# A decayed linear attention in blocks of 64 tokens in place of 128, all its products in 64x64 tiles

## The chip, the cores and the metric

The kernel runs on one core of a Trainium2 chip. The metric is the device time of one execution in microseconds (us); three runs before the change gave 229.84, 229.82 and 229.83, median 229.83. The engines are TensorE (PE, with PEld for its weight loads), VectorE (DVE), ScalarE (ACT), GpSimd (POOL) and SyncE (SP), which issues the transfers. Each takes its instructions in the order in which they were written into the program.

## What is computed

The first half is an attention with an exponential decay per head, 4 batches, 8 heads, 768 tokens, head size 64, as a recurrence over blocks. The reference takes blocks of 64 tokens; the result does not depend on the size of the block.

```python
for b in range(nb):
    qb, kb, vb = (q[:, :, sl], k[:, :, sl], v[:, :, sl])
    intra = np.einsum('bhic,bhjc->bhij', qb, kb) * Dmask[None]
    intra = np.einsum('bhij,bhjd->bhid', intra, vb)
    inter = np.einsum('bhid,bhde->bhie', qb * lam_pow[None], kv_state)
    out[:, :, sl] = intra + inter
    kb_dec = kb * rev_pow[None]
    kv_state = lam_block[None, :, None, None] * kv_state + np.einsum('bhsd,bhse->bhde', kb_dec, vb)
```

The second half takes the attention's result x (the heads side by side, 512 wide): a causal convolution over 5 tokens per channel gives a gate through a sigmoid, x @ w_val is multiplied by the gate, and the product goes through w_out. All is fp32; w_val, conv_w and w_out come as float64.

## The kernel before

The four batches are taken in two pairs, the 768 tokens in 6 chunks of 128: 12 steps, numbered i, of one chunk of one pair each. Steps 0 and 6 begin a pair with an empty state, steps 5 and 11 end one.

A step's recurrence on PE has four kinds of products, all fp32. **Scores** (tile s, line 440): keys times queries for each head and batch, contracting over the head size, in 64x64 tiles of PE with 128 or 64 moving columns, since the upper right quarter is zero and left out; they go in two halves of four heads, u = 0 and 1, through one double bank in PSUM. DVE multiplies each half by the decay mask into A (line 452). **State read** (inter, line 476): the decayed queries qd times the state, 128 columns. **A times v** (intra, line 492): contracting over all 128 tokens of the chunk, so in tiles of 128 rows and 64 columns, into the same xp as the state read. **Outer products** (line 510): decayed keys times v, again over 128 tokens, into st; DVE adds it to the faded state (update, lines 517 and 519), POOL fades the state for the next step into sdec (line 522). In each of them the two batches go side by side. ACT (line 394) or POOL (line 397) scales k, POOL scales q (line 405).

After that, ACT copies xp to x, and x is split into a rounded part x_hi (ACT) and the rest x_lo (DVE in steps 0 and 1, POOL later), so that x @ w_val can be done as three products of a faster type (value groups, tile vp, line 639, 24 products each, two groups a step). DVE does the taps of the convolution (line 603), ACT the sigmoid, DVE multiplies the gate in (line 652), ACT and POOL split again, and PE makes the three products with w_out (output groups, tile op, line 700, 12 products of 512 columns each, two a step). The weights are turned from float64 into such pairs at the start by some ten operations on DVE, ACT and POOL for each half of each weight.

What sets the order is a planner (class Plan): every piece of work is added with an engine, an assumed length, what it needs, the buffers it holds, a rank and, for PE, a number for the tile shape. It plays the work through and writes it out in the order in which the pieces started; the engines then keep to that order. PSUM has eight banks: s and xp two each, four single ones (tag u) for st, the convolution, the value groups and the output groups. A wait in the trace comes from this order together with the semaphores.

Of the kernel before, what the change touches and what calls it, by code (L numbers as in the profile page):

```python
# [9 lines left out]
F32 = mybir.dt.float32  # L10
# [6 lines left out]
P = 128  # L17
C = 128
NB2 = 2
# [4 lines left out]
SLOTS = {"ld": 3, "qd": 2, "A": 2, "x": 3, "xs": 2, "g": 2, "val": 4, "hs": 2, "o": 2, "s": 1, "xp": 1, "u": 4}  # L24
# [5 lines left out]
S_OWN = ()  # L30
# [100 lines left out]
def decay_attention_then_gated_conv(  # L131
# [40 lines left out]
    nc.sync.dma_start(lam_bc, lam.partition_broadcast(P))  # L172
    ident = const.tile([P, P], F32, name="ident")
    make_identity(nc, ident)

    swapped = const.tile([P, P], F32, name="swapped")
    for lo in (0, D):
        nc.gpsimd.tensor_copy(swapped[:, lo : lo + D], ident[:, D - lo : P - lo])
# [11 lines left out]

    dmask = const.tile([P, H, C], F32, name="dmask")

    qdec = const.tile([P, H, C], F32, name="qdec")

    state = const.tile([P, H, D], F32, name="state")
    sdec = const.tile([P, H, D], F32, name="sdec")
    rows = lambda n: slice(n * D, (n + 1) * D)


    s_all = psum.tile([P, NB2, HP, C], F32, name="s", bufs=1)  # L200
    for r in range(2):
        nc.vector.memset(s_all[rows(1 - r), :, 2 * r : 2 * r + 2, 0:D], 0.0)
# [6 lines left out]
    def make_dmask(u):  # L209
        for h in range(HP * u, HP * (u + 1)):  # L210
            nc.vector.tensor_tensor_scan(
                out=dmask[:, h, :],
                data0=lam_bc[:, h : h + 1].to_broadcast([P, C]),
                data1=swapped if h // 2 % 2 else ident,
                initial=0.0,
                op0=ALU.mult,
                op1=ALU.add,
            )

    def make_qdec(h):  # L220
        nc.vector.tensor_tensor_scan(  # L221
            out=qdec[:, h, :],
            data0=lam_bc[:, h : h + 1].to_broadcast([P, C]),
            data1=zero,
            initial=1.0,
            op0=ALU.mult,
            op1=ALU.add,
        )

    t_dmask = {u: add("DVE", 2750, lambda u=u: make_dmask(u), rank=-4 + 0.1 * u) for u in range(2)}  # L230
# [153 lines left out]
    for i in range(N):  # L384
# [16 lines left out]
        def scale_q(u, i=i, s=s):  # L401
            if u == 0:
                s["qd"] = buf("qd", "qd", [P, H, C])
# [363 lines left out]
```

## Time and profile before

| what | value |
|---|---|
| median of 3 runs | 229.83 us |
| span of the profiled execution, first to last instruction | 228.2 us |
| PE busy | 211.4 us, 93% |
| weight load (overlaps PE) | 188.0 us |
| DVE, ACT, POOL busy | 142.8, 112.3, 123.4 us |
| granted PE clock over the span | 0.992 |

In the profile a line names the engine, the operation, the tile written and the tiles read, partitions by elements, the number of instructions, the busy time in us, the mean length of one in ns, and after the second bar the idle time of the engine just before them with what ended it. An fp32 product of the program stands as two matmul records and two weight loads. A record's length reaches over the start of the next ones, so lengths of groups are read from start to start, as the chain of waits gives them. The median is 1.6 us over the span.

### The profile page before, as it was taken

The numbers are of one execution on the slowest core, as the hardware profiler recorded it, in microseconds if no ns is written. First come the engines' busy times: TensorE is split into PE (matmuls) and PEld (weight loads), VectorE is DVE, ScalarE is ACT, GpSimd is POOL, SyncE is SP. The second block draws the span as 40 slices with busy tenths as digits, with TensorE's granted clock in tenths as the row PEclk, the third lists the DMA queues.
The fourth block names the chain that finished last, engine by engine and source line by source line (L and its number), as shares of the span: only waits on it lengthen the run. The fifth ranks groups of instructions, "written<-read, shape, count | busy, mean of one in ns | idle before, by whom it ended". The sixth has DMA issues, their size and how long they took to land.

```text
span 228.2 us, 6134 instructions
## 1 busy us (share of the span) xinstructions
PE 211.4 (93%) x2686; PEld 188.0 (82%) x2686; DVE 142.8 (63%) x196; ACT 112.3 (49%) x190; POOL 123.4 (54%) x93
## 2 busy tenths in 40 slices
PE   7598389997999999999999999999998999999994
PEld 6587388996988999987787899979897899999884
DVE  5598979999799859705789992679117931111100
ACT  2178968458992254254377526455253634121222
POOL 1054997555499989999983224443080616222210
PEclk9999889999999999999999999999999999999999
DMA  5999997997367608183111101111111111111122
GB/s 115 425 418 422 419 399 293 418 375 267 155 217 267 258 3 326 47 329 131 49 49 46 49 0 49 50 46 46 46 47 50 46 46 46 49 46 46 49 92 92
DMA packets 8235, 36.07 MB, mean 158 GB/s; under 512 B 1168, under 2 KB 1424, under 8 KB 4880
## 3 DMA queue, kind: packets, MB, share of 16 engines
q1 hardware_dynamic: 8208, 35.68, 40.4%
q8 instruction: 21, 0.34, 0.6%
q14 instruction: 6, 0.05, 0.1%
HBM read 29.38 MB, written 6.29 MB: 156 GB/s over the span
## 4 chain that ended last, share of the span: by engine, by line
PE 78%; DVE 12%; DMA 2%; ACT 2%; issue 2%; POOL 1%; SPq 0%; ACTq 0%; DVEq 0%
PE vp L639 29%; PE op L700 29%; PE s L440 7%; PE xp L492 7%; DVE A L452 5%; PE xp L476 4%; DVE acc L603 3%; PE st L510 3%; DMA ld<-in_qkv 2%; POOL w_m L283 1%; DVE qdec L221 1%; DVE x_lo L569 1%; DVE w_e L276 1%; ACT g L608 1%; DVE g L652 1%
## 5 line engine op out<-in xcount | busy, mean ns | idle before, releaser
L603 DVE SCALAR_TENSOR_TENSOR acc<-x,conv_sb,acc 128x512 f32<-128x512 f32 x96 | 66.4, 749 | 8.5 <-ACT acc L601 8.3
L700 PE MATMUL op<-wo_hi,hs 128*128 128x512 f32 (+1 forms) x200 | 61.3, 389 | 1.0 <-DVE g L652 0.8
L639 PE MATMUL vp<-x_hi,wv_hi 128*128 128x256 f32 x192 | 54.7, 285 | 0.2 <-ACT g L608 0.2
L639 PE MATMUL vp<-x_hi,wv_lo 128*128 128x256 f32 x192 | 53.6, 279 | 0.0
L639 PE MATMUL vp<-x_lo,wv_hi 128*128 128x256 f32 x192 | 53.6, 279 | 0.0
L677 POOL TENSOR_TENSOR hs<-g,hs 128x512 fp32r<-128x512 f32 x24 | 32.8, 1376 | 33.5 <-ACT hs L674 33.4
L652 DVE TENSOR_TENSOR g<-vp,g 128x512 f32<-128x512 f32 x24 | 16.5, 690 | 46.4 <-PE vp L639 36.1
L700 PEld LDWEIGHTS op<-wo_hi,hs 128*128 128x128 f32 x200 | 35.7, 188 | 8.5 <-DVE g L652 1.0
L708 ACT COPY o<-op 128x512 f32<-128x512 f32 (+1 forms) x25 | 14.2, 569 | 56.1 <-PE op L700 46.9
L574 POOL TENSOR_TENSOR x_lo<-x,x_hi 128x1024 fp32r<-128x1024 f32 x10 | 24.5, 2453 | 30.8 <-ACT x_hi L565 30.8
L700 PE MATMUL op<-wo_lo,hs 128*128 128x512 f32 (+1 forms) x100 | 38.6, 386 | 0.0
L639 PEld LDWEIGHTS vp<-x_hi,wv_hi 128*128 128x128 f32 x192 | 36.0, 187 | 2.5 <-issue 1.0
L639 PEld LDWEIGHTS vp<-x_lo,wv_hi 128*128 128x128 f32 x192 | 36.0, 188 | 0.6
L639 PEld LDWEIGHTS vp<-x_hi,wv_lo 128*128 128x128 f32 x192 | 36.1, 188 | 0.0
L405 POOL TENSOR_TENSOR qd<-ld,qdec 128x512 f32<-128x512 f32 x20 | 26.6, 1348 | 16.4 <-DMA ld<-in_qkv 15.8
L452 DVE TENSOR_TENSOR A<-s,dmask 128x1024 f32<-128x1024 f32 x24 | 29.2, 1218 | 9.8 <-PE s L440 7.5
L440 PE MATMUL s<-ld 64*64 64x128 f32 (+1 forms) x768 | 23.5, 265 | 8.5 <-DVE A L452 7.1
L440 PEld LDWEIGHTS s<-ld 64*64 64x64 f32 x768 | 20.2, 144 | 12.8 <-DVE A L452 8.2
L492 PE MATMUL xp<-A,ld 128*64 128x128 f32 x384 | 28.0, 286 | 2.0 <-DVE A L452 1.2
L492 PEld LDWEIGHTS xp<-A,ld 128*64 128x64 f32 x384 | 22.8, 141 | 4.7 <-issue 1.8
L608 ACT ACTIVATE g<-acc 128x512 f32<-128x512 f32 x24 | 14.3, 597 | 17.9 <-DVE acc L603 17.6
L700 PEld LDWEIGHTS op<-wo_lo,hs 128*128 128x128 f32 x100 | 18.8, 188 | 4.2
(52 smaller groups left out, 220.2 us busy)
## 6 DMA issues: line engine op xcount, KB each, us to landing
ld<-in_qkv SPq DMA_DIRECT2D x22, 1024.0 KB, 8.6
out<-o SPq DMA_DIRECT2D x23, 256.0 KB, 2.0
ld<-in_qkv SPq DMA_DIRECT2D x4, 512.0 KB, 6.6
w_raw<-in_w_val SPq DMA_DIRECT2D x2, 1024.0 KB, 10.8
w_raw<-in_w_out SPq DMA_DIRECT2D x2, 1024.0 KB, 12.4
out<-o SPq DMA_DIRECT2D x2, 128.0 KB, 1.7
conv_raw<-in_conv_w SPq DMA_DIRECT2D x1, 20.0 KB, 7.6
lam_bc<-in_lam SPq DMA_DIRECT2D x1, 4.0 KB, 2.6
```

The costliest lines, as they stand in the source:

```text
L405: nc.gpsimd.tensor_tensor(out=s["qd"][:, hs], in0=lds[i]["qT"][:, u], in1=qdec[:, hs], op=ALU.mult)
L440: nc.tensor.matmul(s_all[keys, b, h, lo:], t["kT"][rows(b), u, h, keys], t["qT"][rows(b), u, h, lo:], start=True, stop=True, skip_group_ch ...
L452: nc.vector.tensor_tensor(out=s["A", u].rearrange("p b h i -> p b (h i)"), in0=s_all.rearrange("p b h i -> p b (h i)"), in1=m.rearrange("p ...
L492: nc.tensor.matmul(s["xp"][rows(h % 2), b, h // 2, :], lds[i]["v"][:, b, h * D : (h + 1) * D], s["A", u][:, b, hl, :], start=first and h < ...
L574: nc.gpsimd.tensor_tensor(out=s["x_lo"], in0=s["x"], in1=s["x_hi"].bitcast(F32), op=ALU.subtract)
L603: nc.vector.scalar_tensor_tensor(out=to, in0=src, scalar=w, in1=to, op0=ALU.mult, op1=ALU.add)
L608: nc.scalar.activation(xu[un]["g"][:, ct].rearrange("p u (b i) -> p b u i", b=NB2), xu[un]["acc", ct].rearrange("p b (u i) -> p b u i", u= ...
L639: nc.tensor.matmul(vp[:, f, :], w[:, ct, fs], xx[:, ct, :], start=n_mm == 0, stop=n_mm == 3 * NT - 1,)
L652: nc.vector.tensor_tensor(out=gs(u), in0=val, in1=gs(u), op=ALU.mult)
L677: nc.gpsimd.tensor_tensor(out=s["h_lo"][:, us], in0=gs(u), in1=s["h_hi"][:, us].bitcast(F32), op=ALU.subtract,)
L700: nc.tensor.matmul(op[:, cols], hh[:, ft, ts], w[:, ft, cols], start=n_mm == 0, stop=n_mm == 3 * NT - 1,)
L708: nc.scalar.copy(s["o", b, j][:, cols], s["op", b, j][:, cols])
```

## The change

The recurrence goes in blocks of 64 tokens. A step is still a chunk of 128 tokens of two batches, but it holds two blocks, k = 0 and 1, and the state is updated, faded and read once for each. All products are 64 by 64 with 64 moving columns: scores only within a block (32 products a step, in one piece but for step 0), outer products per block (32), state read per block (32), A times v per block (32). The data are laid out anew on the host, with half of the heads' batches exchanged, so that four tiles at a time work on different rows and columns of PE. Rows of PE that work side by side write different banks of PSUM. For A times v this needs two turns, z = 0 and 1: tiles of the first turn write one arrangement of banks, those of the second the other, and between them a copy of two columns of xp by ACT (turn) makes the second wait for the first.

In PSUM s, st and xp now share two double banks (tag d). States are three buffers instead of one tile that is overwritten. Steps 0 and 6 read a state too, in their second block; steps 5 and 11 update one, after their first.

```diff
-SLOTS = {"ld": 3, "qd": 2, "A": 2, "x": 3, "xs": 2, "g": 2, "val": 4, "hs": 2, "o": 2, "s": 1, "xp": 1, "u": 4}
+SLOTS = {"ld": 3, "qd": 2, "A": 2, "x": 3, "xs": 2, "g": 2, "val": 4, "hs": 2, "o": 2, "state": 3, "d": 2, "u": 4}
...
-    for h in range(H):
-        t_qdec = add("DVE", 400, lambda h=h: make_qdec(h), [t_qdec], rank=0.4)
+    for a in range(2):
+        t_qdec = add("DVE", 1100, lambda a=a: make_qdec(a), [t_qdec], rank=0.4)
+    t_fadew = add("POOL", 150, make_fadew, [t_qdec], rank=0.4)
...
-                for n in range(2):
-                    for lo in (0, D):
-                        for r in range(2):
-                            h, keys = 2 * r + n, rows(1 - r if lo else r)
+                for a in some:
+                    for p in range(2):
+                        for k in range(2):
+                            for c in range(2):
+                                for b in range(NB2):
+                                    nc.tensor.matmul(
+                                        s["s", n][rows(c), b, k, a, seq(p)],
+                                        kT[rows(b), a, c, p, seq(k)], qT[rows(b), a, c, p, seq(k)],
+                                        start=True, stop=True, skip_group_check=True,
+                                    )
...
+            for k in range(blocks):
+                for n in range(4):
+                    for c in range(2):
                         for b in range(NB2):
                             nc.tensor.matmul(
-                                s["so"][b][:, h], t["kT"][rows(b), u, h], t["qT"][rows(b), u, h], start=True, stop=True
+                                s["st"][rows(b), c, k, n, :], k_[rows(c), k, b, n, :], v_[rows(c), k, b, n, :],
+                                start=True, stop=True, skip_group_check=True,
                             )
...
+        for k in range(blocks):
...
+            t_now = add("DVE", 700, step, [t_st, t_now, t_sdec], [st_buf, new_buf], R - 3, name=f"up{i}")
+            if not (last and k == blocks - 1):
+                t_sdec = add("POOL", 1280, fade, [t_now, t_fadew], [new_buf], R, port=True, name=f"fd{i}")
...
+                                nc.tensor.matmul(
+                                    s["xp"][rows(p), b, 2 * (b ^ c) + a, seq(k)],
+                                    s["state", k][rows(b), c, rows(2 * a + p)], s["qd"][rows(b), a, 2 * c + p, seq(k)],
+                                    start=k == 0 and a == 0 and c == 0, stop=False, skip_group_check=True,
                                 )
...
+        def intra(z, i=i, s=s, first=first, open_xp=open_xp):
+            open_xp()
+            for k in range(2):
+                for n in range(4):
                     for b in range(NB2):
+                        a, p = divmod(n, 2)
                         nc.tensor.matmul(
-                            s["xp"][rows(h % 2), b, h // 2, :],
-                            lds[i]["v"][:, b, h * D : (h + 1) * D],
-                            s["A", u][:, b, hl, :],
-                            start=first and h < 2, stop=h >= H - 2, skip_group_check=True,
+                            s["xp"][rows(p), b, 2 * z + a, seq(k)],
+                            lds[i]["v"][rows(b ^ z), k, b, n, :], s["A"][rows(b ^ z), b, k, a, seq(p)],
+                            start=first and z == 0 and k == 0 and a == 0, stop=z == 1 and k == 1, skip_group_check=True,
                         )
...
+        def change(s=s):
+            nc.scalar.copy(turn, s["xp"][:, :, 0, C - 1])
...
+        t_ia = add("PE", 480, lambda f=intra: f(0), [t_from.get(0), *need], on_xp, R, lag=260, mode=2, name=f"ia{i}0")
...
+        t_turn = add("ACT", 200, change, [t_ia, *t_from.values()], [xp_buf], R - 3, name=f"tn{i}")
+        t_in = [add("PE", 480, lambda f=intra: f(1), [t_turn, *need], on_xp, R, lag=260, mode=2, name=f"ia{i}1")]
```

The planner's table changes with the pieces, so the order changes everywhere. Three places show how.

On PE at the start, from the second step's scores on, before (L440 scores, L510 outer products, L476 state read, L492 A times v):

```order
L510 MATMUL st<-ld 64x64 x16
L440 MATMUL s<-ld 64x128 x4
L440 MATMUL s<-ld 64x64 x4
L440 MATMUL s<-ld 64x128 x4
L440 MATMUL s<-ld 64x64 x4
L476 MATMUL xp<-qd,state 64x128 x16
L492 MATMUL xp<-A,ld 64x128 x8
L510 MATMUL st<-ld 64x64 x16
L492 MATMUL xp<-A,ld 64x128 x8
```

and now (L453 scores, L486 outer products, L547 state read, L563 A times v):

```order
L486 MATMUL st<-ld 64x64 x32
L547 MATMUL xp<-qd,state 64x64 x32
L563 MATMUL xp<-A,ld 64x64 x16
L453 MATMUL s<-ld 64x64 x32
L563 MATMUL xp<-A,ld 64x64 x16
```

The scores of the next step stood ahead of the state read and stand behind it now, between the two turns of A times v.

On PE among the output groups (L700 before, L750 now), one block of recurrence work before:

```order
L700 MATMUL op<-wo_lo,hs 128x512
L492 MATMUL xp<-A,ld 64x128 x8
L510 MATMUL st<-ld 64x64 x16
L492 MATMUL xp<-A,ld 64x128 x8
L440 MATMUL s<-ld 64x128 x4
L440 MATMUL s<-ld 64x64 x4
L440 MATMUL s<-ld 64x128 x4
L440 MATMUL s<-ld 64x64 x4
L700 MATMUL op<-wo_hi,hs 128x512 x2
```

and now:

```order
L750 MATMUL op<-wo_lo,hs 128x512
L547 MATMUL xp<-qd,state 64x64 x32
L563 MATMUL xp<-A,ld 64x64 x16
L486 MATMUL st<-ld 64x64 x32
L563 MATMUL xp<-A,ld 64x64 x16
L750 MATMUL op<-wo_hi,hs 128x512 x2
```

Each row now counts products of the same 64 columns; the outer products are what lies between the two turns of one step.

On POOL in the first stage, before (L405 scales q, L522 fades the state, L283 and L294 belong to the weights):

```order
L522 TENSOR_TENSOR sdec<-state,qdec 128x512
L405 TENSOR_TENSOR qd<-ld,qdec 128x512
L522 TENSOR_TENSOR sdec<-state,qdec 128x512
L283 TENSOR_TENSOR w_m<-w_m,w_raw 128x1024
L405 TENSOR_TENSOR qd<-ld,qdec 128x512 x3
L294 TENSOR_TENSOR wv_lo<-w_m,wv_hi 128x4x256
```

and now (L421, L507, L289, L300):

```order
L507 TENSOR_TENSOR sdec<-state,fadew 128x512
L289 TENSOR_TENSOR w_m<-w_m,w_raw 128x1024
L507 TENSOR_TENSOR sdec<-state,fadew 128x512
L421 TENSOR_TENSOR qd<-ld,qdec 128x512
L507 TENSOR_TENSOR sdec<-state,fadew 128x512
L300 TENSOR_TENSOR wv_lo<-w_m,wv_hi 128x4x256
L289 TENSOR_TENSOR w_m<-w_m,w_raw 128x1024
```

A fade stands on either side of each piece of the weights' work, and the second half of w_val (the second L289) follows right behind the first half, which it did not before.

More of the change, by code (lines that the diff above doesn't have):

```diff
@@ L18 @@
 C = 128
+L = 64
 NB2 = 2
@@ L171, in decay_attention_then_gated_conv @@
     lam_bc = const.tile([P, H], F32, name="lam_bc")
[L172 to L176, printed above, removed]
[L177 to L178 removed]
+    nc.sync.dma_start(lam_bc, lam)
+    whole = const.tile([P, P], F32, name="whole")
+    make_identity(nc, whole)
+    ident = const.tile([P, L], F32, name="ident")
+    nc.gpsimd.tensor_tensor(out=ident, in0=whole[:, 0:L], in1=whole[:, L:P], op=ALU.add)
     zero = const.tile([P, C], F32, name="zero")
@@ new lines, in decay_attention_then_gated_conv @@
+        qd_buf = Buf("qd")
+        t_kd = add(
+            *(("ACT", 1575 * blocks) if i in K_ACT else ("POOL", 1250 * blocks)), scale_k,
+            [t_ld[i, 2], t_ld[i, 3], *t_dmask.values()], [ld_buf[i]], R + RANK["kd"], port=i not in K_ACT, name=f"kd{i}",
+        )
+        t_qd = None
+        for a in range(2):
+            t_qd = add(
+                "POOL", 750 if first else 1300, lambda a=a, f=scale_q: f(a), [t_ld[i, a], t_qdec, t_qd],
+                [ld_buf[i], qd_buf], R + RANK["kd"], port=True, name=f"qd{i}",
+            )
@@ new lines, in decay_attention_then_gated_conv, with update, fade @@
+        if first:
+            states = []
+        def update(k, s=s, states=states):
+            new = buf("state", "state", [P, 2, 4 * D])
+            got = s["st"][:, :, k].rearrange("q c n e -> q c (n e)")
+            if states:
+                nc.vector.tensor_tensor(out=new, in0=got, in1=sdec, op=ALU.add)
+            else:
+                nc.vector.tensor_copy(new, got)
+            states.append(new)
+        def fade(states=states):
+            nc.gpsimd.tensor_tensor(
+                out=sdec.rearrange("q c (n e) -> q (c n) e", n=4),
+                in0=states[-1].rearrange("q c (n e) -> q (c n) e", n=4),
+                in1=fadew.rearrange("q y a p -> q (y a p)")[:, :, None].to_broadcast([P, H, D]), op=ALU.mult,
+            )
@@ L502, in decay_attention_then_gated_conv @@
-        if not last:
-            st_buf = Buf("u")
-            def outer(i=i, s=s):
-                s["st"] = bank("st", [P, H, D])
-                for h in range(H):
-                    hs = slice(h * D, (h + 1) * D)
-                    for b in range(NB2):
-                        nc.tensor.matmul(
-                            s["st"][rows(b), h, :], lds[i]["k"][:, b, hs], lds[i]["v"][:, b, hs],
-                            start=True, stop=True,
-                        )
-            def update(s=s, first=first):
-                if first:
-                    nc.vector.tensor_copy(state, s["st"])
-                else:
-                    nc.vector.tensor_tensor(out=state, in0=s["st"], in1=sdec, op=ALU.add)
-            def fade():
-                nc.gpsimd.tensor_tensor(
-                    out=sdec, in0=state, in1=qdec[:, :, C - 1 : C].to_broadcast([P, H, D]), op=ALU.mult
-                )
-            t_st = add("PE", 1200, outer, [t_kd], [st_buf, ld_buf[i]], R, lag=260, mode=3, name=f"st{i}")
-            t_state = add("DVE", 700, update, [t_st, t_read, t_sdec], [st_buf], R - 3, name=f"up{i}")
-            t_sdec = add("POOL", 1280, fade, [t_state, t_qdec], [], R, port=True, name=f"fd{i}") if (i + 2) % NC else None
```

245 lines of the change are left out of this document (130 added, 115 removed).

## The prediction

> **What bounds the kernel now.** I read the page's totals first, then the slices, then the windows, cut where one thing gives way to another, and last the chain of waits.
>
> ```profile
> span 228.2 us, 6134 instructions
> PE 211.4 (93%) x2686; PEld 188.0 (82%) x2686; DVE 142.8 (63%) x196; ACT 112.3 (49%) x190; POOL 123.4 (54%) x93
> ...
> PEclk9999889999999999999999999999999999999999
> ```
>
> The span is 228.2 us, and the three runs have 229.83 as their median (229.82 to 229.84), so 1.6 us lie around the span; I make my sum as a difference to this execution and take it off 229.83. A PE of 93% says that TensorE matters most on the average, not where. The windows below end where the fourth value group (vp) has ended, where the recurrence is nearly done, and where PE has done its last product. Columns are the stretch, its length, then the busy time of PE, weight load, DVE, ACT and POOL, the granted clock and the DMA share.
>
> ```profile
> 0.00:62.75 62.75, 51.44 (x996) 47.28 (x998) 52.88 (x77) 41.74 (x84) 33.79 (x33) 0.97 0.86 337
> 62.75:129.80 67.05, 66.10 (x1065) 57.53 (x1065) 51.08 (x63) 33.09 (x47) 57.21 (x40) 1.00 0.40 147
> 129.80:225.20 95.40, 93.88 (x632) 83.19 (x628) 38.81 (x57) 37.09 (x61) 32.43 (x21) 1.00 0.13 51
> 225.20:228.20 3.00, 0.00 (x0) 0.00 (x0) 0.00 (x0) 0.37 (x1) 0.00 (x0) 0.99 0.23 81
> ```
>
> Up to 62.75 PE is idle for 11.3 us and DVE busy for 52.9: a latency stage, in which the chain runs over DVE, loads and PE in turn. From 62.75 to 225.2 PE is idle for 2.5 us of 162.45. There PE is the bound, and what a recurrence step costs on PE is paid in full. The last 3.0 us are the last output's copy and store.
>
> **The change part by part.** The price of each kind of product comes from the chain, where a piece lasts from its start to the start of the next one (start, length, what).
>
> ```profile
> 85.15 0.83 PE s L440 x32
> 85.98 3.02 PE vp L639 x24
> ...
> 89.83 0.88 PE xp L476 x32
> ...
> 93.74 1.07 PE xp L492 x16
> ...
> 202.78 2.82 PE vp L639 x24
> ...
> 30.49 1.08 PE st L510 x32
> ```
>
> How many of them lie after 62.75 comes from the groups of that stretch:
>
> ```profile
> L492 PE MATMUL xp<-A,ld 128*64 128x128 f32 x208 | 14.8, 280 | 1.2 <-DVE A L452 1.2
> L440 PE MATMUL s<-ld 64*64 64x128 f32 (+1 forms) x384 | 10.8, 250 | 0.0
> L510 PE MATMUL st<-ld 128*64 128x64 f32 x160 | 5.8, 224 | 0.0
> L476 PE MATMUL xp<-qd,state 64*64 64x128 f32 x160 | 5.4, 272 | 0.0
> ```
>
> An fp32 product of the program is two records. So there are 384/32 = 12 groups of scores at 0.83, 160/32 = 5 of state read (the L476 lines) at 0.88 to 1.03 (I take 0.95, since half of them follow a group of another tile shape), 208/16 = 13 of A times v at 1.07 and 160/32 = 5 of outer products at 1.08: 10.0 + 4.75 + 13.9 + 5.4 = **34.0 us of recurrence after 62.75**.
>
> *All products in 64x64 tiles.* In the changed program's order the fourth value group is followed by 192 score products, 208 of state read, 224 of A times v and 144 outer products, together 768, which is 24 groups of 32. All have 64 moving columns and come four tiles at a time, so 32 products are 64 records in 16 waves of four. The trace has no long run of such waves, so I bound one. From below: the state read has four tiles and 128 columns, 32 records in 8 waves, 0.88/8 = 0.110 us a wave; half the columns, 0.055. From above, as far as the tiles go: the outer products have 64 columns in two tiles, 16 waves in 1.08, 0.067 each with their start-up in it. I take 0.060, between the two and nearer the row with the same number of tiles. A group is then 16 x 0.060 = 0.96 us and 24 groups 23.0 (21.1 to 25.7). That removes 34.0 - 23.0 = **11.0 us** (8.3 to 12.9), all on the path, since PE is the bound there.
>
> *Fewer changes of tile shape.* A value group lasts 3.02 after the recurrence and 2.82 after an output group: 0.20 for coming back from small tiles. After the fourth value group the order before comes back 17 times, the new one 13 times: 4 x 0.20 = **0.8 us** gained (0 to 1.6).
>
> *The copy between the two turns.* The second turn of A times v waits for ACT to read two columns of xp. The nearest row for such a copy is 0.20, and the instruction most often in front of it on ACT is the copy to x at 1.01:
>
> ```profile
> L183 ACT ACTIVATE preload<-zero 128x1 f32<-128x1 f32 x1 | 0.2, 203 | 0.0
> L541 ACT COPY x<-xp 128x1024 f32<-128x1024 f32 x12 | 12.1, 1012 | 7.2 <-PE xp L492 7.2
> L394 ACT ACTIVATE ld<-ld,dmask 128x128 f32<-128x128 f32 x48 | 14.7, 392 | 8.6 <-DMA ld<-in_qkv 8.6
> ```
>
> PE is not idle meanwhile where the order puts something between the turns: a value or an output group (2.8 us) covers it, one group of 32 (0.96) covers it not quite. After the fourth value group three steps have only such a group. The wait there is 1.01 + 0.20 + two hand-overs of 0.04 - 0.96 = 0.33 each, **1.0 us** lost in all. Bounds: nothing, and 5 us if the eight scalings of k stand ahead of it each time (8 x 0.392 = 3.1, of which 1.7 not covered). What is queued behind on PE is everything, since it takes its work in order; behind the copy on ACT stands the copy to x, which needs the second turn anyway.
>
> *Masks, updates, fades.* Per step one mask in place of two, two state updates in place of one, two fades on POOL in place of one; the scans have half the columns.
>
> ```profile
> L452 DVE TENSOR_TENSOR A<-s,dmask 128x1024 f32<-128x1024 f32 x24 | 29.2, 1218 | 9.8 <-PE s L440 7.5 <-PE xp L492 2.2
> L522 POOL TENSOR_TENSOR sdec<-state,qdec 128x512 f32<-128x512 f32 x8 | 9.5, 1191 | 2.8 <-DVE state L519 1.4 <-DVE state L517 1.3
> L519 DVE TENSOR_TENSOR state<-st,sdec 128x512 f32<-128x512 f32 x8 | 5.5, 685 | 0.9 <-PE st L510 0.8
> L221 DVE TENSOR_TENSOR_SCAN qdec<-lam_bc,zero 128x128 f32<-128x128 f32 x8 | 3.9, 536 | 0.0
> ```
>
> DVE gets 12 x (1.22 - 0.69) = 6 us less, POOL 14 more fades at 1.19 = 17 us more, and some 5 for scaling q in each pair's first step and k in its last. In the PE-bound stages both have room on their sums: POOL is busy for 57.2 of 67.05 and then for 32.4 of 95.4, so 22 more make 112 of 162. I cost them at nothing there; the cover is PE's own queue of value and output groups.
>
> *The stage to 62.75* is where they cost or gain. Both orders have done four value groups and the scores of six steps at its end. Its masks are
>
> ```profile
> L452 DVE TENSOR_TENSOR A<-s,dmask 128x1024 f32<-128x1024 f32 x12 | 14.6, 1217 | 4.2 <-PE s L440 2.7 <-PE xp L492 1.4
> ```
>
> Those twelve, 14.6 us, become five and two halves, 7.4. Five updates become ten, +3.5. Of sixteen scans, half as long in columns, at most half the time goes, 16 x 0.54/2 = 4.3; I take 2.0. So DVE has 5.7 less to do, which is the gain if DVE alone were the limit. Against that the state now passes a fade and a second update within a step, 1.19 + 0.69, with no overlap inside the chain: five steps, +9.4 if none of it is hidden. PE's recurrence there falls from 31.9 to 21.1 us (11 groups of A times v, the others as many as after 62.75; then 704 products, 22 groups of 0.96), yet that only adds to its idle time. Between -5.7 and +9.4 I take **+1.0**, a little below the middle, since some of the fades end while a load is awaited. An idle PE also lost its clock once:
>
> ```profile
> 24.00:27.40 3.40, 0.91 (x34) 0.77 (x34) 3.40 (x4) 3.40 (x10) 3.40 (x3) 0.91 1.01 419
> 27.40:31.00 3.60, 3.60 (x83) 3.43 (x85) 3.60 (x5) 3.08 (x7) 3.60 (x3) 0.61 1.03 428
> ```
>
> After 3.4 us with 0.91 busy the granted clock was 0.61 in the next stretch. A second time of that kind costs up to 1.4 us of PE work and is inside the bounds just given.
>
> **Sum:** 11.0 + 0.8 - 1.0 - 1.0 = 9.8 us off 229.83: **220.0 us**.
>
> **The rivals.**
>
> *The whole of PE's saving is kept* (15%). If the value groups could fill PE's idle time in the first stage, all of the recurrence counts: 24 groups of scores, 10, 24 and 10 of the others are 19.9 + 9.5 + 25.7 + 10.8 = 65.9 before, and 1472 products, 46 groups of 0.96, are 44.2 after: 21.7, and 22 changes of shape fewer, 2.2. That is 206. For it speaks that the second half of w_val is fetched earlier in the new order; against it that PE waits 11.3 us in that stage already, and its waits are for loads and for DVE.
>
> *The first stage grows* (16%). The state chain shows in full, +9.4 in place of +1.0: 228.4. For it speaks that PE, DVE and POOL each take their work in order, and the new order on PE has the read of the state ahead of the next scores; against it that the chain needs 2 x (0.69 + 1.19) = 3.8 us a step and a step's load of 2 MB, at the 420 GB/s of the clock windows above, needs 5.
>
> *Records, not columns, set the pace* (12%); this one ends slower. In the trace no group on PE goes below 0.83/32 = 0.026 us a record, whatever its tiles and columns: that may be the sum of the columns, as I take it, or the pace at which PE can start records. In the latter case 64 records take 1.66 us, 24 groups 39.9 in place of 34.0, +5.9, and the first stage has 1408 records, 36.6 for 31.9, of which I count half, +2.4; with the other terms 229.8 + 5.9 + 2.4 - 0.8 + 2.0 = 239. It decides from 1.37 us a group on (21 ns a record), where nothing is left of the gain. For my case speaks that 64-column scores are part of the 0.83 and the 128-column read costs more than it, 0.88; a fixed pace would make them equal.
>
> The Trainium skill, page "TensorE: Matmul & The Clock Gate", section "Wait — 56ns, not 53.3ns?", speaks for this rival: start to start does not fall below about 25 ns a matmul, however few columns. By that a group of 64 records would be 1.6 us, and the 24 groups 4.4 us dearer than now; the trace's 26 ns does not contradict it, and the page does not say whether tiles side by side count apart.
>
> *The change does nothing here* (3%): the saving is eaten by new waits to within 0.2%, about what a measurement of this kernel can tell from no change.
>
> **How the numbers follow.** My forecast has 54%. Faster by over 0.2%: 54 + 15 + 15 of the second rival's 16, **0.84**. Slower: 12 + 1, **0.13**; the same **0.03**. The range starts at the full saving, 206, and goes up to 229, which takes in the first stage's upper bound together with the upper price of a wave; outside lie the slow rival and a few better cases.
>
> **What would show it.** A group of 32 products of any of the four kinds at 0.9 to 1.05 us in the chain proves the wave, 1.4 or more the slow rival. The fourth value group should end at 58 to 68 us; earlier than 55 speaks for the full saving. From there to PE's end 162.45 should become about 151.6 (162.45 - 11.0 - 0.8 + 1.0), with idle time before the second turn of three steps only. POOL should read 140 to 150 us busy, DVE 132 to 138. If PE is idle for more than 8 us after the fourth value group, with updates or fades as releasers, the step that I cost at nothing was wrong.

## Result and profile after

The changed kernel takes **255.07 us** (median of four runs, 254.50 to 255.94) against 229.84 (229.82 to 230.23): a ratio of 1.108, with a 95% interval of 1.104 to 1.113. I had predicted 220.0, faster. The profiled execution took 254.5, with a span of 252.7.

The page of the changed kernel: totals, granted clock by slices, the instruction queues' transfers, and the shares of the chain of waits.

```profile
span 252.7 us, 8463 instructions
PE 209.7 (83%) x3838; PEld 186.8 (74%) x3838; DVE 138.1 (55%) x195; ACT 113.5 (45%) x202; POOL 140.8 (56%) x111
...
PEclk9756855597999999988999997999999999999999
...
q8 instruction: 30, 0.49, 0.8%
...
PE 63%; issue 12%; POOL 10%; DVE 6%; DMA 3%; ACT 2%; SPq 1%; POOLq 0%; ACTq 0%; DVEq 0%
```

The same of the kernel before, its queue q8 and its chain:

```profile
q8 instruction: 21, 0.34, 0.6%
...
PE 78%; DVE 12%; DMA 2%; ACT 2%; issue 2%; POOL 1%; SPq 0%; ACTq 0%; DVEq 0%
```

PE is busy about as long as before (211.4) in a span that is 24.5 us longer. "issue", time in which an engine waits for nothing that the chain can name, holds 12% of the chain, 31 us; before it was 2%. Of the 31 us, 10.3 are one wait of POOL, which the view of waits below does name. And the clock was down in the first third.

The windows of the changed kernel, first the two longest stretches at half clock, then cut where the fourth value group has ended and where PE has done its last product:

```profile
9.30:23.00 13.70, 8.44 (x275) 7.67 (x270) 5.40 (x10) 7.85 (x23) 5.81 (x7) 0.50 0.93 377
29.80:50.30 20.50, 13.08 (x352) 12.25 (x353) 12.12 (x12) 11.79 (x21) 10.91 (x8) 0.50 0.64 244
0.00:79.84 79.84, 52.82 (x1526) 48.75 (x1529) 48.39 (x77) 40.67 (x87) 42.15 (x41) 0.76 0.65 245
79.84:249.70 169.86, 156.88 (x2316) 138.09 (x2316) 89.70 (x118) 72.40 (x114) 98.64 (x70) 0.98 0.26 97
```

So the first stage went from 62.75 to 79.84 us (+17.1), with 27.0 us of PE idle in it (79.84 - 52.82; 11.3 before). The rest of PE's work went from 162.45 to 169.86 (+7.4), with 13.0 idle (2.5 before). I had forecast 63.75 and 151.6.

The chain of waits of the changed kernel (start, length, what) has the groups near the price that I predicted, where nothing stops them:

```profile
134.08 1.09 PE s L453 x64
...
138.17 1.09 PE xp L547 x64
139.26 0.47 PE xp L563 x32
...
143.37 0.93 PE st L486 x64
```

64 records in 0.93 to 1.09 us, 58 to 68 ns a wave of four. But in the same chain PE stops in the middle of such groups:

```profile
28.04 0.41 PE s L453 x10
28.45 2.85 issue
31.30 1.66 PE s L453 x51
...
43.15 2.37 issue
...
68.73 0.34 PE xp L563 x21
69.07 2.71 issue
71.78 0.44 PE xp L563 x11
...
150.17 2.49 issue
```

Nothing is awaited there: products of one group, with one wait at its head, stand on both sides. With three shorter ones (0.51 to 0.82) these stops add up to 12.5 us. The trace's transfers show pieces of the instruction queue q8, 16 KB each, starting at 28.90, 43.24, 69.37 and 150.16, and PE goes on 2.3 to 2.5 us after each. PE has 2 x 3838 = 7676 matmul and weight-load instructions and the queue brought 30 pieces; in the kernel before it is 2 x 2686 = 5372 and 21. Both are 256 to a piece, that is 128 matmul records with their weight loads. And the stops stand at the ends of pieces: counted in matmul records from the start, the seven begin after 476, 730, 985, 1113, 1367, 2387 and 2897, at distances of one, two, eight and four times 127 to 128.

The other waits, in the view of who waited for whom, PE after 68 us and then POOL after 62 us (in total, times, longest, in us):

```profile
PE st L486 <- POOL ld L410: 3.7, 1, 3.7
PE xp L563 <- ACT turn L570: 1.4, 1, 1.4
...
POOL sdec L507 <- DVE state L501: 14.6, 4, 10.3
POOL sdec L507 <- DVE state L503: 5.2, 1, 5.2
```

POOL, which takes its work in order, sits for 10.3 us behind one fade whose state DVE has not written, and then has some 20 us of other work in its order before the scaling of k that PE awaits (its wait ends at 111.67).

### The profile page after: what moved, and what is told of

The parts are those of the page before. It is cut to its first block, busy times and chain, and to the rows that moved or that the text cites. A ratio compares the mean times of both kernels' runs of the same rounds, so it can differ in the third digit from the quotient of the medians.

```text
span 252.7 us, 8463 instructions
## 1 busy us (share of the span) xinstructions
PE 209.7 (83%) x3838; PEld 186.8 (74%) x3838; DVE 138.1 (55%) x195; ACT 113.5 (45%) x202; POOL 140.8 (56%) x111
## 4 chain that ended last, share of the span: by engine, by line
PE 63%; issue 12%; POOL 10%; DVE 6%; DMA 3%; ACT 2%; SPq 1%; POOLq 0%; ACTq 0%; DVEq 0%
PE op L750 27%; PE vp L689 20%; PE st L486 5%; PE s L453 4%; PE xp L547 4%; DMA ld<-in_qkv 3%; PE xp L563 3%; POOL w_m L289 2%; POOL sdec L507 2%; DVE A L463 2%; POOL hs L727 1%; DVE acc L653 1%; POOL x_lo L624 1%; POOL qd L419 1%; POOL qd L421 1%
## 5 line engine op out<-in xcount | busy, mean ns | idle before, releaser
L750 PE MATMUL op<-wo_hi,hs 128*128 128x512 f32 (+1 forms) x200 | 63.2, 399 | 2.9 <-DVE g L702 0.8
L727 POOL TENSOR_TENSOR hs<-g,hs 128x512 fp32r<-128x512 f32 x24 | 31.6, 1330 | 35.3 <-ACT hs L724 35.3
L750 PEld LDWEIGHTS op<-wo_hi,hs 128*128 128x128 f32 x200 | 36.9, 193 | 11.8 <-DVE g L702 1.2
L702 DVE TENSOR_TENSOR g<-vp,g 128x512 f32<-128x512 f32 x24 | 16.5, 689 | 52.0 <-PE vp L689 34.3
L507 POOL TENSOR_TENSOR sdec<-state,fadew 128x512 f32<-128x512 f32 x20 | 22.5, 1123 | 36.0 <-DVE state L501 27.2
L758 ACT COPY o<-op 128x512 f32<-128x512 f32 (+1 forms) x25 | 14.2, 569 | 57.2 <-PE op L750 44.4
L750 PE MATMUL op<-wo_lo,hs 128*128 128x512 f32 (+1 forms) x100 | 39.2, 392 | 0.0
L421 POOL TENSOR_TENSOR qd<-ld,qdec 128x512 f32<-128x512 f32 x20 | 26.5, 1329 | 4.4 <-DMA ld<-in_qkv 4.4
L563 PE MATMUL xp<-A,ld 64*64 64x64 f32 x768 | 19.8, 243 | 8.7 <-issue 5.2
L453 PE MATMUL s<-ld 64*64 64x64 f32 x768 | 16.7, 242 | 11.5 <-issue 6.5
L453 PEld LDWEIGHTS s<-ld 64*64 64x64 f32 x768 | 14.9, 155 | 13.3 <-issue 9.3
L563 PEld LDWEIGHTS xp<-A,ld 64*64 64x64 f32 x768 | 16.7, 155 | 10.4 <-issue 6.6
L463 DVE TENSOR_TENSOR A<-s,dmask 128x1024 f32<-128x1024 f32 (+1 forms) x13 | 14.7, 1140 | 16.5 <-PE s L453 16.3
L486 PE MATMUL st<-ld 64*64 64x64 f32 x704 | 17.5, 260 | 7.0 <-POOL ld L410 3.7
```

Of the source, the lines that this page charges most:

```text
L421: nc.gpsimd.tensor_tensor(out=s["qd"][:, a].rearrange("q n (b i) -> q n b i", b=2), in0=q.rearrange("q n (b i) -> q n b i", b=2), in1=by[: ...
L453: nc.tensor.matmul(s["s", n][rows(c), b, k, a, seq(p)], kT[rows(b), a, c, p, seq(k)], qT[rows(b), a, c, p, seq(k)], start=True, stop=True, ...
L463: nc.vector.tensor_tensor(out=pick(s["A"]), in0=pick(s["s", n]), in1=m[:, :, None, :].to_broadcast([P, NB2, 2, w * 2 * L]), op=ALU.mult,)
L486: nc.tensor.matmul(s["st"][rows(b), c, k, n, :], k_[rows(c), k, b, n, :], v_[rows(c), k, b, n, :], start=True, stop=True, skip_group_check ...
L507: nc.gpsimd.tensor_tensor(out=sdec.rearrange("q c (n e) -> q (c n) e", n=4), in0=states[-1].rearrange("q c (n e) -> q (c n) e", n=4), in1= ...
L563: nc.tensor.matmul(s["xp"][rows(p), b, 2 * z + a, seq(k)], lds[i]["v"][rows(b ^ z), k, b, n, :], s["A"][rows(b ^ z), b, k, a, seq(p)], sta ...
```

## The experiments

Six theories, by the letters that the expectations use. **F**: PE is supplied with only some 256 instructions in 3.5 us, and runs of recurrence groups use them up faster. **C**: the lost clock. **H**: scores, st and xp wait for each other in the two shared double banks, and the state chain is longer. **M**: POOL stands behind fades that come late. Later **P**, the assumption of the prediction that PE alone is the bound after the first stage, against **B**: POOL's and DVE's queues are nearly as full there. The first eight kernels were timed once each and stand beside the time of the kernel before on the same chip, 228.56 for the first four and 229.65 for the next four; repeated executions of one kernel lie up to 1.5 us on either side of their median below, so a gain of 2 us in a single one is not clear.

**PE alone.** The kernel's work is left out; PE issues 640 products of 64 columns in four tiles, 320 of 128 columns in four tiles, and 320 of 64 columns in two tiles.

```diff
+    for n in range(160):
+        for c in range(2):
+            for b in range(NB2):
+                nc.tensor.matmul(s4[rows(c), b, 0:D], data[rows(b), 0:D], data[rows(b), D : 2 * D], ...)
+    for n in range(80):   # 128 columns: l4[rows(c), b, 0:C] <- data[rows(b), 0:C]
+    for n in range(160):  # two tiles: s4[rows(b), b, D : 2 * D]
```

> A measurement by itself: PE alone, no waits, three stretches one after the other: 640 products of 64x64 tiles, four tiles at a time, with 64 moving columns; 320 with 128 columns; 320 in two tiles with 64 columns. Nothing of the kernel's computation is in it. Theory F (PE runs out of instructions: they come in pieces of 256, and the changed kernel's recurrence uses them up at some 140 a us): the first stretch does not hold 0.057 us a wave; it shows stops of 0.5 to 2.5 us about once in 256 instructions, and takes over 24 us in place of 18.4 (320 waves at 0.0575); the second (73 instructions a us) and third (69) run with next to no stops at 0.110 and 0.058 a wave. Rival (the stops in the changed kernel have another cause, as transfers in the way): 18 to 19.5 us for the first stretch, without stops.

The chain of that run: two rounds of the first stretch, then the second and the third:

```profile
10.38 2.09 PE s L198 x128
12.48 1.64 issue
14.11 2.09 PE s L198 x128
...
42.57 14.36 PE l L205 x512
...
58.64 18.72 PE s L211 x637
```

No other engine works and the clock is full, yet PE stops after every 128 records. From 10.38 to 39.12 there are eight rounds, 3.59 us each: **28 ns a record, 14 ns an instruction**, where the records between the stops take 2.09/128 = 16 ns. 512 records of 128 columns take 14.36, also 28 ns each, with no stop; 637 records in two tiles 29 ns. So 64 columns in four tiles ask for instructions at 1.7 times the rate at which they come, and gain nothing over 128 columns or two tiles in a long run. F is shown for PE alone. From the start of a piece's transfer to PE's next product it takes 2.2 to 2.7 us in these rounds, more than the 2.09 us that 128 records last in a burst and less than the 3.59 us that they last at 28 ns.

The changed kernel has no run as long as this one. Before each of its four long stops the last transfer had started 5.4 to 9.7 us earlier, so there it is not the round of 3.59 us that binds: PE has used up a piece when the transfer of the next one is only starting, and why it starts so late is not shown.

The Trainium skill, page "TensorE: Matmul & The Clock Gate", section "Wait — 56ns, not 53.3ns?", has start to start not below about 25 ns; by the trace tiles side by side start every 16 ns in a burst, and only the sustained rate, 28 ns, is near that figure.

**Half the instructions.** Pairs of products become one of 128 columns: as many columns, half as many instructions, and a computation that is no longer the reference's.

```diff
-for p in range(2): ... matmul(s["s", n][rows(c), b, k, a, seq(p)], kT[rows(b), a, c, p, seq(k)], qT[rows(b), a, c, p, seq(k)])
+matmul(s["s", n][rows(c), b, k, a, :], kT[rows(b), a, c, 0, seq(k)], qT[rows(b), a, c, k, :])
 ... (the same in st, in the state read and in A times v)
```

> Each pair of products with 64 columns in the recurrence becomes one with 128 columns, in the same order, tiles, buffers and waits: half of PE's recurrence instructions for the same PE time (0.110 in place of 2 x 0.057 a wave pair). The attention is no longer computed, half of the stationary operands are left out. Theory F: the chain's issue share falls from 12% (31 us) to under 6%, and the time by 8 to 14 us to 241 to 247. Theory C (the granted clock) and theory H (hops between the engines through the shared banks): 252 to 257, since neither is touched.

236.29, below what F had said (241 to 247): 17 us of the 25 are back. No such stop is left in its chain. The share of "issue" is still 7%, 16 us, but 10.0 of it is again one wait of POOL. Its windows, cut as above:

```profile
0.00:67.40 67.40, 47.78 (x822) 41.25 (x822) 48.76 (x77) 40.65 (x87) 42.80 (x41) 0.80 0.77 294
67.40:231.40 164.00, 153.33 (x1549) 133.02 (x1548) 89.46 (x119) 72.47 (x114) 98.71 (x70) 0.99 0.26 97
```

The first stage is 12.4 us shorter, the rest 5.9. Some of it is not supply: its groups take 0.87 to 1.03 us in place of 0.93 to 1.09, and 46 groups at 0.06 are 2.8 us. What stays is 10.7 us of PE idle in the second stretch.

**No fades.** POOL's fades are left out; the update adds the last state itself, so the result is another.

```diff
-            nc.gpsimd.tensor_tensor(out=sdec..., in0=states[-1]..., in1=fadew..., op=ALU.mult)
+            pass
-                nc.vector.tensor_tensor(out=new, in0=got, in1=sdec, op=ALU.add)
+                nc.vector.tensor_tensor(out=new, in0=got, in1=states[-1], op=ALU.add)
```

> The fades of the state on POOL are left out and the update adds the state itself, in the same order otherwise; the decay between blocks is not computed. Theory H: the state's chain loses a hop to POOL in every block; the fourth value group ends at 66 to 72 us in place of 79.8, POOL no longer sits idle for 10 us behind a fade in the middle, and the time falls to 238 to 247. Theories F and C: less than 4 us gained, 251 to 255.

251.11, where the changed kernel would have 253.7 on this chip (255.07 x 228.56/229.84), so less than 3 us, as F and C had said; the first stage ends at 78.9. Twenty operations of 1.1 us and their hop in the state chain are not where the time went, as long as the instruction stops are there. POOL's long wait comes back for a part of w_out (7.8 us).

**PE kept busy.** Nine products on zeros (the expectation says ten), 512 columns each, after seven groups of the first stage, for the clock's sake.

```diff
+    for name, n in {"ia00": 1, "s1": 1, "st0": 1, "st1": 2, "s2": 1, "ia11": 1, "st2": 2}.items():
+        plan.extra[name] = lambda n=n: keep_pe(n)   # n x matmul(keep, zero, wide)
```

> Ten products of zeros with 512 columns are put into PE's order in front of the waits of the first 35 us; all else stays, the result too. Theory C: the granted clock up to 60 us rises from about 0.67 to over 0.9, the recurrence's groups there fall from 2.0 to 1.1 us, the fourth value group ends by 72 us in place of 79.8, and the time falls to 244 to 249. Theory H: the clock rises, but the waits for DVE and POOL take the place of the slow groups: the fourth group ends at 77 to 82, time 251 to 257.

250.98, again less than 3 us. Its first stage:

```profile
0.00:74.40 74.40, 57.37 (x1544) 45.60 (x1544) 49.54 (x78) 40.95 (x87) 42.82 (x41) 0.89 0.70 263
```

The clock rises from 0.76 to 0.89, not to full, and the stage ends 5.4 us earlier, at 74.4, between the two expectations, but the rest takes 171.7 in place of 169.9. The clock is the smaller part of the loss.

**The kernel before, in pieces of 64 columns.** No block of 64, no turn, no shared bank, no second fade: each product of 128 columns is issued as two of 64.

```diff
-s_all[keys, b, h, lo:] <- qT[rows(b), u, h, lo:]
+for at in range(lo, C, D): s_all[keys, b, h, at : at + D] <- qT[rows(b), u, h, at : at + D]
 ... (the same for the state read and A times v)
```

> The kernel before with one thing changed: each product of the recurrence with 128 moving columns is issued as two with 64. Same result, same tiles, banks, waits, DVE and POOL work; 128 products a step in place of 80, as many as the changed kernel has (PE instructions 5372 to about 7700). Theory F (PE is fed at 256 instructions in some 3.5 us): 240 to 252, with stops on PE that nothing else explains. Rivals (the state's chain, the clock, the shared banks; none of which is in this kernel): 229 to 232, the extra being 1 to 2 us for the shorter columns.

**254.28** against 229.65, as slow as the changed kernel. But not all of it is F. Its chain has half a step of A times v at

```profile
78.76 1.47 PE xp L496 x32
```

in place of 1.07, where products in a row now stand in one tile; 24 x 0.40 = 9.6 us of PE work, by estimate, are that. It was repeated with the tiles alternating:

```diff
-for b in range(NB2): for at in (slice(0, D), slice(D, C)): matmul(...)
+for at in (slice(0, D), slice(D, C)): for b in range(NB2): for hl in (2 * g, 2 * g + 1): matmul(...)
```

> The kernel before with each 128-column product of the recurrence issued as two of 64 columns, as in the run before of that kind, but ordered so that products next to each other use different tiles. F (the number of PE instructions in a row costs, through their supply): A times v no dearer than 1.2 us a half step, yet PE stops inside runs of recurrence groups in the first stage, the fourth value group ends at 70 to 76 in place of 62.7, time 238 to 247. Price only (the earlier run was slow because of two products in a row in one tile): 229 to 235, no more stops than before.

247.23, a ratio of 1.077 (1.067 to 1.086), at the upper end of what F had said. Its chain:

```profile
43.27 0.75 PE s L441 x40
44.03 0.90 PE xp L497 x25
44.93 3.51 issue
48.44 0.69 PE xp L497 x7
...
54.19 1.08 PE xp L497 x32
```

and its windows:

```profile
0.00:76.90 76.90, 58.59 (x1524) 54.34 (x1526) 53.60 (x77) 42.45 (x84) 33.73 (x34) 0.87 0.73 276
76.90:241.60 164.70, 161.36 (x2253) 143.74 (x2252) 89.89 (x119) 70.02 (x106) 88.32 (x60) 1.00 0.24 90
```

A times v is now no dearer (1.08), yet the fourth value group ends at 76.9 in place of 62.75, 14.2 of the 16.5 us by which the profiled span is longer. After it, where value and output groups stand between the recurrence groups, the same change costs only 2.3. Of the 14.2 us PE is idle for 7.0 (18.3 in place of 11.3); the other 7.1 are longer busy time, at a clock of 0.87 in place of 0.97, and whether the stops brought the clock down is not shown. The stops inside groups again stand at the ends of pieces: the one of 3.51 us begins after 987 records, the next two after 1242 and 1369. So more instructions for the same columns, 5372 to 7548 with nothing else changed, make the kernel before slow, and in the stage that is dense in them.

**Two at a time.** Half the instructions with PE kept busy, then half the instructions with the late update that POOL waits for moved forward in DVE's order, then that move alone.

```diff
+        first, late = [k for k in dve if self.names[k] == "up6"]
+        dve.remove(late)
+        dve.insert(dve.index(first) + 3, late)
```

> Half the recurrence's instructions (as in the second run) and the ten products of zeros (as in the fourth) together. Where the instructions are out of the way, theory C says that the clock is what is left in the first stage: the fourth value group ends at 60 to 64 us in place of 67.4, the time is 230 to 233 against 236.3. If the loads and the chain set the stage: 66 to 69 and 235 to 238.

> Half the recurrence's instructions, and one DVE instruction moved: the second state update of step 6 stands two taps behind the first, in place of fourteen instructions later; the orders of PE, POOL and ACT stay. Theory M (POOL sits for 10 us at a fade behind that update while the weights of w_out and the scaling of k wait behind it): POOL's longest wait for the state falls from 10.0 to under 3 us, PE's idle time after the fourth value group from 10.7 to 4 to 6 us, the time from 236.3 to 229 to 232. If POOL's wait is hidden: 235 to 237.

> The changed kernel with the moved update alone, all instructions there. Theory M: 4 to 7 us less than the changed kernel's 253.7 on this chip (255.07 x 228.56/229.84): 247 to 250. If the instruction supply takes the place of the wait: 252 to 254.

234.71, 235.51 and 257.43 us. Half the instructions alone are 237.4 on this chip's scale (236.29 x 229.65/228.56), so the clock is worth 2.7 us and the move 1.9, neither of them clear in a single execution. The windows with half the instructions and PE kept busy:

```profile
0.00:64.90 64.90, 51.96 (x840) 39.05 (x840) 48.55 (x78) 40.63 (x87) 43.93 (x41) 1.00 0.79 301
64.90:229.80 164.90, 154.43 (x1549) 133.79 (x1548) 89.50 (x119) 72.46 (x114) 98.81 (x70) 0.98 0.27 98
```

The first stage then ends at 64.9, about where the prediction had it (63.75) and between the two expectations. The move missed what M had said in both runs. With half the instructions POOL's wait came back under another name:

```profile
POOL w_m L320 <- ACT w_m L306: 10.0, 1, 10.0
```

Freed from the fade, POOL waits as long for the next thing in its order, a part of w_out that DVE and ACT have not got to yet. In the changed kernel itself the move gains nothing (257.43, where it would have 254.9 on this chip). M in its first form, one misplaced update, fell.

**Is PE alone the bound after the first stage?** In the kernel before, six of the eight products with x_lo are left out of 16 value groups after the fourth: 96 x 0.118 = 11.3 us of PE, the size of the gain that I forecast there. Then the same, with POOL's eight splits into x_lo left out too (PE reads x_hi for it).

```diff
 for w, xx in ((wv.hi, x_hi), (wv.hi, x_lo), (wv.lo, x_hi)):
+    if xx is x_lo and 2 <= i < 10 and ct > 0:
+        continue
 ...
 def split_x_lo(...):          # the second run alone
+    if 2 <= i < 10: return
```

> The kernel before; in the value groups of steps 2 to 9 (16 groups, all after the fourth value group) six of the eight products with x_lo are left out, nothing else: the split into x_lo is still made, the order is the same. 96 products at 2.82/24 = 0.118 us are 11.3 us of PE work, as much as I had the recurrence save there. P (what the prediction assumed: after the fourth value group PE alone is the bound): all of it is kept, 229.7 - 11.3 = 218.4, PE idle after the fourth value group stays at 2 to 3 us. B (POOL's and DVE's queues are as full there as PE's, so a shorter PE has to wait for them): less than two thirds are kept, 222 to 226, PE idle there 6 to 10 us between 63 and 120 us, released by POOL and DVE.

> The same kernel with the same products left out on PE, and in steps 2 to 9 POOL's split into x_lo as well (eight operations of 2.4 us, 19.6 us); the two products left in each group read x_hi in its place, so PE does exactly what it does in the run with fewer value products. P: the same time as that run, within 1 us. B: 3 to 7 us less than that run, near 218 to 220, PE idle after the fourth value group back to 2 to 4 us.

221.69 and 218.53 against 229.34 (ratios 0.966, 0.956 to 0.976, and 0.952, 0.949 to 0.956). Their second windows, in this order:

```profile
62.75:129.80 67.05, 62.39 (x1024) 53.05 (x1022) 53.44 (x64) 32.76 (x47) 56.89 (x42) 1.00 0.41 147
```

```profile
62.75:129.80 67.05, 66.10 (x1056) 57.11 (x1053) 53.75 (x69) 35.15 (x50) 44.37 (x36) 1.00 0.41 151
```

Of 11.3 us taken from PE, 7.7 are gained, and 10.8 when POOL has less to do: with POOL at 56.9 of 67.05 PE is idle for 4.7 us, with POOL at 44.4 for 0.9. The two intervals only just miss each other, with two executions of each; the idle times say the same. B holds, at a smaller size than I expected of it: I had 6 to 10 us idle and less than two thirds kept, and for the second run 3 to 7 us more, where it is 3.2. PE's longest waits in the first of them are for POOL's scaling of q (1.5 us) and for its second part of w_out (1.3).

**What is left without the instruction limit.** Half the instructions with POOL's splits into x_lo left out in steps 2 to 11; half the instructions with st in two single banks of its own; and all three causes lessened at once (half the instructions, PE kept busy, no splits).

```diff
-        st_buf = Buf("d")
+        st_bufs = [Buf("u"), Buf("u")]
-            s["st"] = bank("st", [P, 2, 2, 4, D], "d")
+            s["st"] = [bank("st", [P, 2, 4, D]) for c in range(2)]
```

> The changed kernel with half as many recurrence products of twice the columns (as in the run with half the instructions, 236.3), and POOL's split into x_lo left out in steps 2 to 11 (ten operations, 24.8 us; the value groups read x_hi twice). B (what is left of the loss without the instruction limit is POOL standing late in the stretch after the fourth value group): PE idle there falls from 10.7 to 3 to 5 us, the time to 229 to 232. H (the shared double banks): POOL is not what PE waits for, 235 to 237.

> The changed kernel with half as many recurrence products of twice the columns (236.3), and st in two single banks of tag u in place of a shared double bank. H (st, the scores and xp wait for each other in two shared double banks): 229 to 233, PE idle after the fourth value group 10.7 -> 4 to 7. B: 235 to 238, idle 9 to 12, since POOL is as late as before.

> The changed kernel with half as many recurrence products of twice the columns, PE kept busy in the first stage (nine products on zeros) and POOL's split into x_lo left out in steps 2 to 11, that is with all three found causes taken away or lessened. If they are the whole of the miss: the fourth value group ends at 62 to 65 and the time is 220 to 228. If something of its own is left in the new form (the longer state chain, the turn): 229 to 233, with PE idle after the fourth value group above 6 us.

232.26 (on this chip half the instructions would be 237.1), 257.50 and 230.96 us, the last against 229.62, a ratio of 1.007 (1.002 to 1.011). Less POOL is worth 4.8, near what B had said (229 to 232). But its second stretch is

```profile
66.60:226.70 160.10, 151.54 (x1549) 131.94 (x1548) 86.97 (x119) 72.37 (x114) 75.85 (x61) 1.00 0.27 101
```

and PE's idle time there falls only from 10.7 to 8.6, where B had 3 to 5: so most of that idle time is not POOL's splits. The single banks miss both theories: taken from the value groups, the convolution and the output groups, they cost 20 us. In that run's waits PE stands for the gate:

```profile
PE vp L687 <- ACT g L656: 11.3, 4, 6.3
```

So it tells nothing on what the sharing costs; the kernel has no bank to spare for it. With all three causes lessened the windows are

```profile
0.00:65.50 65.50, 51.22 (x840) 38.53 (x844) 48.65 (x78) 40.61 (x87) 41.46 (x40) 0.95 0.79 300
65.50:226.60 161.10, 153.44 (x1548) 133.22 (x1548) 86.94 (x119) 72.50 (x114) 75.89 (x61) 0.99 0.27 100
```

and the longest wait of PE after the first stage, in the view of who waited for whom:

```profile
PE xp L565 <- ACT turn L572: 2.5, 1, 2.5
```

The time does not come down to 220 to 228, as it should have if these three were all. It is what was expected if the new form has a cost of its own (229 to 233, with over 6 us of PE idle; 7.7). POOL's wait of 10.0 us for a late state is still in this run, so POOL was only relieved, not freed.

## Why the prediction was wrong

| | to the end of the 4th value group | from there to PE's end |
|---|---|---|
| before | 62.75 | 162.45 |
| forecast | 63.75 | 151.6 |
| changed | 79.84 | 169.86 |
| half the instructions | 67.4 | 164.0 |
| ... and PE kept busy | 64.9 | 164.9 |
| ... and less POOL | 65.5 | 161.1 |

*The price of a wave* was nearly right for a group by itself: 0.93 to 1.09 us where nothing stops PE (I took 0.96). Over the whole second stretch the 24 groups hold PE for 27.3 us, 1.14 each, in part at half clock; I had 23.0, at most 25.7. *But the sum multiplied this price of a single group by 24 and 22 groups, and left out that the program now holds more instructions.* The step goes from 80 products to 128, PE's instructions from 5372 to 7676. They come in pieces of 256, and PE stops when it has used up one before the next is there: 12.5 us of such stops stand in the chain. Over a long run they come at 14 ns each, at which a group of 64 records lasts 64 x 28 = 1.8 us. That is the term that was missing. It is what the third rival claimed, with the place of its price wrong: I judged it by single groups, where it is false (15 ns a record), and it holds over a run of them. It had named 1.37 us a group as the point from which the gain is lost. Taking the instructions away gives 12.4 + 5.9 us back, of which 2.8 are a lower price of a group; giving them to the kernel before costs 17.6.

*The first stage, taken at +1.0,* cost +17.1. I had costed it by DVE's sum and by the state chain, and called PE's share there something that "only adds to its idle time". It is where recurrence groups follow each other with hardly a value group between them, so where the instructions run out. With these stops gone and the clock kept, the stage is +2.2 (64.9). The bounds of the state chain (-5.7 to +9.4) were wide enough for that; the missing term was outside them.

*The clock.* I allowed 1.4 us for a second loss. The two long stretches at half clock hold 8.44 + 13.08 = 21.5 us of PE work, but the two runs that kept PE busy gained only 2.7 us each in all, though the stage by itself became 5.4 and 2.5 shorter.

*"All on the path, since PE is the bound there"* was wrong by about a third, as the shortened kernel before shows (7.7 of 11.3 kept). I read POOL's 57.2 of 67.05 as room. Three finer windows of the kernel before would have told more:

```profile
62.75:80.00 17.25, 16.32 (x327) 15.06 (x328) 16.15 (x22) 8.36 (x12) 17.15 (x13) 1.00 0.67 246
80.00:100.00 20.00, 20.00 (x318) 18.73 (x317) 12.93 (x11) 8.46 (x11) 19.31 (x10) 1.00 0.41 144
100.00:120.00 20.00, 20.00 (x250) 16.11 (x250) 12.20 (x17) 10.52 (x17) 18.95 (x16) 1.00 0.31 122
```

Until 120 us POOL is nearly as full as PE. A PE that gets ahead there waits for POOL: in the shortened kernel before for the scaling of q and the second part of w_out, in the changed kernel for the scaling of k (3.7) and x_lo (0.9).

*Fades "at nothing"*: the sign that I named for their failing came in its number, 13.0 us of PE idle after the fourth value group, but only in part in its releasers. The scaling of k that stands behind a late fade is 3.7 of them and the instruction stops are 3.3. Leaving the fades out gained less than 3 us, and moving the late update gained nothing, so what the fades cost by themselves is small or stays open.

*The turn,* +1.0, was 2.0 in the changed kernel's trace and 3.2 with all three causes lessened (2.5 in one step). The casts in front of it on ACT, in the run with all three lessened:

```profile
83.55 1.04 ACT L302 CAST wo_hi<-w_m 128x1024 fp32r<-128x1024 f32 x1
84.49 1.05 ACT L617 CAST x_hi<-x 128x1024 fp32r<-128x1024 f32 x1
85.43 0.16 ACT L572 COPY turn<-xp 128x2 f32<-128x2 f32 x1
```

Two casts stood before it, not one copy; the upper bound (5 us) held. *Fewer changes of tile shape,* +0.8, counted too much: by PE's records the kernel before goes from the recurrence to a value or output group 11 times after the fourth value group, the new one 13 times. The 17 comes out only with the changes between the two kinds of small tiles, whose price no run shows. *POOL and DVE busy* came about as worked out: 140.8 (140 to 150) and 138.1 (132 to 138).

The second stretch can be divided by PE's records, each instant given to the record started last. In the changed kernel it is 18.3 us over the forecast: 9.5 of idle time, 4.6 of recurrence, 4.1 of value and output groups. With all three causes lessened it is still 9.5 us over: idle 7.7 in place of 2.5 + 1.0, so 4.2; recurrence 25.5 in place of 33.6 - 11.0, so 2.9; value and output groups 127.9 in place of 126.3 - 0.8, so 2.4, with 3.4 us at half clock in it. Part of the idle time is the turn; how the rest divides between the shared banks, the longer state chain, POOL's order and PE's was not told apart, so this part of the miss stays open. No version tried beats the kernel before, apart from those that leave work out.

## What to carry to other kernels

Count PE's instructions beside its columns: cutting products into smaller tiles can make a group cheaper and a run of groups dearer, and a price read from one group does not give the price of a run. Before a saving on the busiest engine is taken in full, look at windows short enough to show whether a second engine is as full there; an average over a long stage hides it. And an engine that is idle for part of a stage (PE in the first one) can still come to lengthen it, if the change adds to what that engine has to wait for.

## What was not expected of the hardware

- PE's instructions arrive in pieces of 16 KB, 256 of them, one every 3.59 us in a long run with nothing else on the chip's engines: 14 ns an instruction, 28 ns for a matmul with its weight load, and PE stops for 1.3 to 1.6 us after each 128 records if these take 16 ns. In the changed kernel the four long stops begin within 0.5 us of the start of a piece's transfer and last 2.4 to 2.9 us.
- The clock stays at half for four and six times 3.4 us (13.70 and 20.50 above) although PE is busy for 62% and 64% of these windows; 18 records on zeros, 10.5 us of work, brought the stage to 1.00 with half the instructions; with all of them, to 0.89. The Trainium skill, page "TensorE: Matmul & The Clock Gate", section "Part 1: The HAM clock gate (the "warmup" mystery)", has a free-running window of about 3.4 us; the lengths agree with it.
- Two products in a row in one tile of 128 rows and 64 columns cost 1.47 us for 32 records of 64 columns, alternating tiles 1.08.
